# Attention and a bilinear feed-forward layer on one core: the turns of q and k as 64x64 products in four quarters of TensorE

## The chip, the cores and the metric

One core of one Trainium2 chip. The metric is the device time of one execution in microseconds (us). Before the change the median of three runs is 1480.76 us, the lowest 1478.62, the highest 1485.36.

A core has engines that run side by side: TensorE (PE in the profile, with its weight loads listed apart as PEld), VectorE (DVE), ScalarE (ACT), GpSimd (POOL) and the sync engine (SP), whose queue here issues most of the DMAs. A matrix product takes a stationary operand, loaded first, and a moving operand that streams through; its result goes to PSUM, from where another engine copies it.

## The reference

Batch 8, 12 heads, sequence 448, head width 64; then a feed-forward layer over 3584 rows of 768, with inner width 1536.

```python
q_n, k_n = (rmsnorm(q, g_q), rmsnorm(k, g_k))          # over the head width
scores = scale * np.matmul(q_n, k_n.transpose(0, 1, 3, 2))
attn = softmax(scores)                                  # written out in the reference
attn_out = np.matmul(attn, v)
x = attn_out.transpose(0, 2, 1, 3).reshape(3584, 768)
out = ((x @ w_a) * (x @ w_b)) @ w_out
```

q, k, v and the gains are fp32. The three weight matrices are double precision in memory; the kernel loads their words and rounds them itself.

## The kernel before, in words

The program is a list of operations that a planner class (`Plan`) collects and then emits. The order in which they are emitted is written out in a packed constant, `ORDER`; the engines and costs given with each operation are not used to choose an order at build time. Each engine then works through its own instructions in that order and waits on semaphores where it needs another's result.

**Attention.** The work comes in 24 groups `p`: each has four heads of one batch element, as two pairs `w`, each of two heads `h`. For a group, q and k are loaded into tiles of 128 partitions: the pair `w` fills partitions 0 to 63 or 64 to 127 (`low_high[w]`), and each partition holds seven tokens of each head (`NT` = 7 blocks `j` of 64 features). `loads` (L411 on) issues two DMAs a tile on SP, one for each pair; for group 0 one half goes on the ACT queue (L432). q lies as head, then block; k, before the change, as block, then head, so that for every `j` the 128 columns of both heads stand side by side.

`normalize` squares q and k on ACT (L461), adds up on DVE (L463), and takes the inverse root on POOL (L498). q is multiplied by it on DVE (`apply`, L502) into `qn`, which before the change lies as block, then head, like k. k's factor is applied later, as the scale of the exponential (L591).

`transposes` (L523 on) turns k and q so that the head width lies on the partitions. For every block `j` one transpose of 128x128 on TensorE (L537) moves four 64x64 squares (two pairs, two heads), so a turn is seven transposes. The result stands in PSUM in two banks, and ACT copies it to `qkT` (L542 for k, L544 for q with the gain). Group 0 does the same in `turn_first` (L561, L566, L568), with q in two parts and with products on the identity (`warm`, L408) between them, which compute nothing.

`scores` (L585) makes, for each of seven blocks of keys, four products of 64 keys by 448 queries, one in each quarter of the array (64 rows by 64 columns), and ACT takes the exponential into `ET`. `values` (L607) multiplies `ET` by v, again in quarters. The sums over keys come from products with ones (L643), after additions on DVE and POOL (L621) for the later groups.

**Feed-forward.** Between and after the attention, the products with the weights run on the full array (L1292, L869, L1190, L993), on matrices that DVE and ACT combine from the rounded weights (L247 to L256, `factors`). The tiles of k and q are also lent to this part under the same tags (`dF`, `ti`), so their shape appears there again.

The waits of a turn: it needs its input (k's DMA or `qn`), a free `sc` slot in PSUM (two exist, shared with the scores), and so the exponential that reads the slot's last content.

Of the kernel before, what the change touches and what calls it, by code (L numbers as in the profile page):

```python
# [147 lines left out]
def kernel(  # L148
# [126 lines left out]
    def fast_body(ld, wk, ps_s, ps_o, ps_mm, dram):  # L275
# [7 lines left out]
        STS, XS = 2, 9  # L283
        WARM, SPLIT = 4, ((0, 4), (4, NT))
# [129 lines left out]
        def loads(p, nm):  # L414
            b, h0 = p // HC, 4 * (p % HC)
            src = {"q": q, "k": k, "v": v}[nm]
            t = tile_of(f"{nm}{p}", nm, 2 if nm == "v" else 1)

            def emit():
                x = ld.tile([P, NT, 2, D] if nm == "k" else [P, 2, NT * D], FP32, tag=nm, name=nm + "_sb", bufs=2 if nm == "v" else 1)  # L420
                for w in range(2):
                    pair = src[b, h0 + 2 * w:h0 + 2 * w + 2]
                    nc.sync.dma_start(x[low_high[w]], pair.rearrange("h (p j) d -> p j h d" if nm == "k" else
                                                                     "h (p j) d -> p h (j d)", j=NT))
                xs[nm, p] = x
            if p == 0 and nm != "v":
                def begin():
                    xs[nm, p] = ld.tile([P, NT, 2, D] if nm == "k" else [P, 2, NT * D], FP32, tag=nm, name=nm + "_sb", bufs=1)

                def half(w):  # L430
                    pair = src[b, h0 + 2 * w:h0 + 2 * w + 2]
                    queue[("SP", "ACT")[w]].dma_start(  # L432
                        xs[nm, p][low_high[w]], pair.rearrange("h (p j) d -> p j h d" if nm == "k" else "h (p j) d -> p h (j d)", j=NT))
                op(None, 0.0, -11, begin, [], [f"{t}/{w}" for w in range(2)], new=[t])
                for w in range(2):
                    op(("SP", "ACT")[w], 0.7, -10, lambda w=w: half(w), [], [f"{t}/{w}"], kb=350)
                return
            op("SP", 1.28 if nm != "k" else 1.4, p - (1.8 if nm == "v" else 2.0), emit, [f"firsts{PREP}"] if p >= HELD else [], [t], new=[t],
               kb={"q": 690, "k": 770, "v": 530}[nm], dmas=2)
# [4 lines left out]
        def normalize(p):  # L444
# [8 lines left out]
            def squares(s, nm):  # L453
                sq = tile_of(f"sq{nm}{p}", "sq", 1)

                def square():
                    x = xs[nm, p]
                    t = xs["sq", nm, p] = wk.tile([P, 2 * NT, D], FP32, tag="sq", name="sq")
                    flat = (x.rearrange("p h (j d) -> p (h j) d", d=D) if nm == "q" else
                            x.rearrange("p j h d -> p (j h) d"))  # L460
                    nc.scalar.activation(t, flat, AF.Square)  # L461
                op("ACT", 0.95, key, square, loaded(p, nm), [sq], new=[sq])
                op("DVE", 1.1, key, lambda: nc.vector.tensor_reduce(rs[p][:, s], xs["sq", nm, p], AX, ALU.add), [sq], [f"{ms}/{nm}"])  # L463

            def front(n):
# [10 lines left out]
                def times():  # L476
                    if n == 0:
                        qns[0] = wk.tile([P, NT, 2, D], FP32, tag="qn", name="qn")
                    nc.vector.tensor_tensor(
                        qns[0][:, j0:j1].rearrange("p j h d -> p h j d"),  # L480
                        xs["q", 0][:, :, j0 * D:j1 * D].rearrange("p h (j d) -> p h j d", d=D),
                        rs[0][:, 0, a:c].rearrange("p (h j) -> p h j ()", h=2).to_broadcast([P, 2, j1 - j0, D]), ALU.mult)
# [17 lines left out]
            def apply():  # L500
                qns[p] = wk.tile([P, NT, 2, D], FP32, tag="qn", name="qn")
                nc.vector.tensor_tensor(  # L502
                    qns[p].rearrange("p j h d -> p h j d"),
# [19 lines left out]

        def transposes(p):
# [5 lines left out]
            for n, nm in ((1, "k"), (0, "q")):  # L530
                pt = tile_of(f"pt{nm}{p}", "sc", 2)

                def turn(n=n):
                    t = pts[p, n] = ps_s.tile([P, 2 * 512], FP32, tag="sc", name="pt")
                    x = xs["k", p] if n == 1 else qns[p]
                    for j in range(NT):
                        nc.tensor.transpose(t[:, j * P:(j + 1) * P], x[:, j].rearrange("p h d -> p (h d)"), ident)  # L537

                def take(n=n):
                    if n == 1:  # L540
                        qkTs[p] = wk.tile([P, 2, 2 * S], FP32, tag="qkT", name="qkT", bufs=2)
                        nc.scalar.copy(qkTs[p][:, 1], pts[p, 1][:, 0:2 * S])  # L542
                    else:
                        nc.scalar.activation(qkTs[p][:, 0].rearrange("p (w j t) -> p w j t", w=2, j=NT),  # L544
                                             pts[p, 0][:, 0:2 * S].rearrange("p (j w t) -> p w j t", w=2, j=NT),
                                             AF.Copy, scale=gain[:, 0:1])
                op("PE", 0.75, key, turn, [f"{nm}{p}" if n else f"qn{p}", f"half{p - 1}"], [pt], new=[pt], mode="full")
                op("ACT", 0.91 if n else 1.01, key, take, [pt, "gain"], [f"{qkT}/{n}"], new=[qkT] if n else [])

        def turn_first():  # L550

            tile_of("qkT0", "qkT", 2)
            for nm, j0, j1, n in (("k", 0, NT, None), ("q", *SPLIT[0], 0), ("q", *SPLIT[1], 1)):
# [3 lines left out]
                def turn(nm=nm, j0=j0, j1=j1, n=n):  # L557
                    t = pts[0, n] = ps_s.tile([P, 2 * 512], FP32, tag="sc", name="pt")
                    x = xs["k", 0] if n is None else qns[0]
                    for j in range(j0, j1):  # L560
                        nc.tensor.transpose(t[:, (j - j0) * P:(j - j0 + 1) * P], x[:, j].rearrange("p h d -> p (h d)"), ident)  # L561

                def take(j0=j0, j1=j1, n=n):
                    if n is None:
                        qkTs[0] = wk.tile([P, 2, 2 * S], FP32, tag="qkT", name="qkT", bufs=2)
                        nc.scalar.copy(qkTs[0][:, 1], pts[0, None][:, 0:2 * S])  # L566
                    else:
                        nc.scalar.activation(qkTs[0][:, 0].rearrange("p (w j t) -> p w j t", w=2, j=NT)[:, :, j0:j1],  # L568
                                             pts[0, n][:, 0:(j1 - j0) * P].rearrange("p (j w t) -> p w j t", w=2, j=j1 - j0),
                                             AF.Copy, scale=gain[:, 0:1])  # L570
                op("PE", 0.95 * size, -9, turn, (loaded(0, "k") if n is None else [f"qn0/{n}"]) + ["heat"], [pt, "heat"], new=[pt], mode="full")
# [5 lines left out]
        def scores(p, j):  # L577
# [3 lines left out]
            def product():  # L581
                t = scs[p, j] = ps_s.tile([P, 2, 512], FP32, tag="sc", name="sc")
                for w in range(2):
                    for e in range(2):
                        nc.tensor.matmul(t[low_high[w], e, 0:S], lhsT=qkTs[p][low_high[e], 1, j * P + w * D:j * P + (w + 1) * D],  # L585
                                         rhs=qkTs[p][low_high[e], 0, w * S:(w + 1) * S], start=True, stop=True)

            def exps():
                E = ETs[p, j] = wk.tile([P, 2, S], FP32, tag="ET", name="ET", bufs=4)
                for e in range(2):  # L590
                    nc.scalar.activation(E[:, e], scs[p, j][:, e, 0:S], AF.Exp,  # L591
                                         scale=rs[p][:, 1, 2 * j + e:2 * j + e + 1])
# [215 lines left out]
        def deep_products(beta, key, names, h):  # L808
# [30 lines left out]
            def step(m, f, F, names_F):  # L839
# [44 lines left out]
                def first():  # L884
                    pool_, shape = {"k": (ld, [P, NT, 2, D]), "sq": (wk, [P, 2 * NT, D])}.get(tag, (ld, [P, 2, NT * D]))
                    t = pool_.tile(shape, FP32, tag=tag, name="dF", **({"bufs": bufs} if pool_ is ld else {}))
                    F[f] = t.rearrange("p a b c -> p (a b c)" if tag == "k" else "p a b -> p (a b)")
# [224 lines left out]
        def inner_factors(beta, f):  # L1112
# [5 lines left out]
            for k in (slice(0, MI - 1), slice(MI - 1, MI)):  # L1118
                size = (k.stop - k.start) * HI
                quarter = lambda i, j, k=k: (lambda: sts[beta, at][:, i * MI + k.start:i * MI + k.stop, j * HI:(j + 1) * HI])  # L1120
                made = lambda n: (lambda: ts[n])
                for n, x, y, reads in ((2, quarter(1, 1), quarter(0, 1), []), (0, quarter(0, 1), quarter(0, 0), []),
# [3 lines left out]
                    def emit(n=n, x=x, y=y, k=k, size=size):  # L1126
                        t = wk.tile([P, S], FP32, tag="t", name="tk", bufs=2)
                        ts[n] = t[:, 0:size].rearrange("p (k n) -> p k n", n=HI)
                        nc.vector.tensor_tensor(ts[n], x(), y(), ALU.subtract)
                    op("DVE", 0.16 + size / 980, -0.5, emit, [st] + [f"tk{f}.{x}.{k.start}" for x in reads], [nm, "inner factors"], new=[nm], lock=True)  # L1130
                    op("SP", 0.38, 0, lambda n=n, k=k: nc.sync.dma_start(kept["t"][:, f, n, k], ts[n]), [nm], [f"kt{f}.{n}.{k.start}"], kb=0.42 * size)
# [3 lines left out]
        def stream_inner(beta, f):  # L1135
            for n in range(4):
# [3 lines left out]
                def load(n=n, tag=tag, bufs=bufs):  # L1140
                    shape = {"ET": [P, 2, S], "k": [P, NT, 2, D]}.get(tag, [P, 2, NT * D])
                    t = (wk if tag == "ET" else ld).tile(shape, FP32, tag=tag, name="ti", bufs=bufs)
                    flat = t.rearrange("p a b c -> p (a b c)" if tag == "k" else "p a b -> p (a b)")
# [427 lines left out]
```

## Time and profile before

| | |
|---|---|
| median of three runs | 1480.76 us |
| the profiled execution | 1483.82 us |
| its span (first to last instruction) | 1482.0 us |
| TensorE busy | 1459.8 us, 98% of the span, 7886 matmul instructions |
| VectorE, ScalarE, GpSimd busy | 987.5, 437.9, 323.0 us |
| turns of groups 1 to 23 (L537) | 322 matmul instructions |
| DMA packets | 188883, of them under 512 B 62564 |

Busy time of TensorE is the union of instructions in flight; since they are pipelined, their throughput is read from the distance of starts, not from their durations. In the timeline an entry such as `x7` merges seven instructions; its first number is the start of the first and the second the time to the end of the last. A square bracket tells how long the engine stood idle before, and what ended that.

### The profile page before, as it was taken

To read this page: it belongs to the slowest core of one execution; us is meant where nothing else is said; L and a number is where in the kernel's file an instruction comes from. 1 tells how busy PE (TensorE), PEld (TensorE's weight loads), DVE (VectorE), ACT (ScalarE), POOL (GpSimd) and SP (SyncE) were. 2 spreads that over 40 slices of the span, in tenths; PEclk is the share of its full clock that TensorE was granted. 3 is DMA by queue.
4 is the path that set the end of the run, shared out by engine and by line. 5 is a ranking of instruction groups with operands and counts; after the bars stand their busy time and mean duration, and the time that the engine had idled before them with its cause. 6 is when DMAs were issued, how large, how long until landed. Compare 5 with 4: busy or idle time off the path is not lost.

```text
span 1482.0 us, 21059 instructions
## 1 busy us (share of the span) xinstructions
PE 1459.8 (98%) x7886; PEld 960.0 (65%) x7886; DVE 987.5 (67%) x1575; ACT 437.9 (30%) x792; POOL 323.0 (22%) x175
## 2 busy tenths in 40 slices
PE   8999999999999999999999999999999999999998
PEld 5433444555445555555544445799998899999898
DVE  5987799888766233334658765467677766776786
ACT  5878652111464000000257771011111011111100
POOL 3336541120233001101155551011120001111000
PEclk9999999999999999999999999999999999999999
DMA  9885567554443455554656544555555755555464
GB/s 226 221 235 168 123 164 210 187 186 169 159 120 89 155 170 161 178 170 149 180 156 154 128 132 149 165 170 155 161 168 180 251 172 166 159 151 158 160 197 144
DMA packets 188883, 247.99 MB, mean 167 GB/s; under 512 B 62564, under 2 KB 161380, under 8 KB 182116
## 3 DMA queue, kind: packets, MB, share of 16 engines
q1 hardware_dynamic: 159652, 192.61, 45.4%
q10 hardware_dynamic: 29120, 53.94, 10.9%
q8 instruction: 65, 1.06, 0.3%
q14 instruction: 46, 0.38, 0.1%
HBM read 188.35 MB, written 57.93 MB: 166 GB/s over the span
## 4 chain that ended last, share of the span: by engine, by line
PE 84%; DVE 2%; DMA 1%; issue 0%; ACT 0%; SPq 0%; DVEq 0%
PE pq L1292 24%; PE dg L869 17%; PE po L993 16%; PE da L869 6%; PE o L607 5%; PE sc L585 5%; PE a L1190 2%; PE g L1190 2%; PE pt L537 1%; PE b L1190 1%; PE e L1190 1%; PE d L1190 1%; PE su L643 1%; DMA ti<-kept_t 1%; DMA kept_o<-st 0%; DVE x L736 0%
## 5 line engine op out<-in xcount | busy, mean ns | idle before, releaser
L1292 PE MATMUL pq<-x,st 128*128 128x448 f32 x1008 | 384.8, 542 | 2.5 <-DVE t L1333 2.4
L1292 PEld LDWEIGHTS pq<-x,st 128*128 128x128 f32 x1008 | 190.9, 191 | 191.9 <-issue 177.2
L591 ACT ACTIVATE ET<-sc,ms 128x448 f32<-128x448 f32 x336 | 191.0, 637 | 80.3 <-PE sc L585 63.6
L498 POOL TENSOR_TENSOR ms<-ms,expo 128x14 f32<-128x14 f32 x47 | 141.0, 3003 | 117.6 <-DVE ms L496 103.6
L869 PE MATMUL dg<-dT,st 128*128 128x224 f32 x672 | 165.1, 353 | 0.0
L993 PE MATMUL po<-st,hT 128*128 128x384 f32 x492 | 164.2, 488 | 0.0
L869 PE MATMUL dg<-x,st 128*128 128x224 f32 x672 | 163.3, 353 | 0.2 <-DVE dF L916 0.2
L585 PE MATMUL sc<-qkT 64*64 64x448 f32 x1344 | 153.1, 543 | 6.4 <-ACT ET L591 3.4
L607 PE MATMUL o<-ET,v_sb 64*64 64x448 f32 x1344 | 149.3, 540 | 0.0
L897 POOL TENSOR_TENSOR hT<-dF 128x448 f32<-128x448 f32 x42 | 47.1, 1136 | 423.1 <-DVE dF L892 323.0
L993 PEld LDWEIGHTS po<-st,hT 128*128 128x128 f32 x492 | 92.6, 190 | 64.4 <-issue 4.6
L869 PEld LDWEIGHTS dg<-x,st 128*128 128x128 f32 x672 | 126.6, 190 | 2.4 <-DVE dF L916 1.2
L869 PEld LDWEIGHTS dg<-dT,st 128*128 128x128 f32 x672 | 126.6, 190 | 1.4 <-issue 0.2
L621 POOL TENSOR_TENSOR sum<-sum,ET 128x896 f32<-128x896 f32 x40 | 89.0, 2225 | 159.8 <-DVE sum L621 83.2
L869 PE MATMUL da<-x,st 128*128 128x224 f32 x504 | 118.4, 353 | 0.0
L585 PEld LDWEIGHTS sc<-qkT 64*64 64x64 f32 x1344 | 46.3, 132 | 89.8 <-issue 41.3
L607 PEld LDWEIGHTS o<-ET,v_sb 64*64 64x64 f32 x1344 | 49.8, 133 | 72.7 <-issue 64.5
L869 PEld LDWEIGHTS da<-x,st 128*128 128x128 f32 x504 | 94.5, 190 | 1.1
L892 DVE TENSOR_TENSOR dF<-dF 128x896 f32<-128x896 f32 x84 | 92.9, 1106 | 2.5
L621 DVE TENSOR_TENSOR sum<-sum,ET 128x896 f32<-128x896 f32 x60 | 65.3, 1088 | 35.5 <-POOL sum L621 29.2
L882 ACT COPY dt<-da 128x224 f32<-128x224 f32 x84 | 29.1, 346 | 197.5 <-PE da L869 87.1
L993 PE MATMUL po<-st,fin 128*128 128x384 f32 x252 | 86.7, 492 | 0.0
(151 smaller groups left out, 1663.8 us busy)
## 6 DMA issues: line engine op xcount, KB each, us to landing
st<-kept_o SPq DMA_DIRECT2D x28, 1152.0 KB
st<-kept_s SPq DMA_DIRECT2D x84, 320.0 KB
kept<-st ACTq DMA_DIRECT2D x12, 1344.0 KB
st<-kept SPq DMA_DIRECT2D x12, 1344.0 KB
st<-kept SPq DMA_DIRECT2D x84, 192.0 KB
ti<-kept_t SPq DMA_DIRECT2D x48, 288.0 KB
kept_s<-ds SPq DMA_DIRECT2D x30, 448.0 KB
v_sb<-in_v_dram SPq DMA_DIRECT2D x48, 224.0 KB
```

The lines of the kernel that those rows point to most:

```text
L498: lambda: nc.gpsimd.tensor_tensor(msf(), msf(), expo[:, 0:2 * NT * (b - a)], ALU.pow), [], names)
L585: nc.tensor.matmul(t[low_high[w], e, 0:S], lhsT=qkTs[p][low_high[e], 1, j * P + w * D:j * P + (w + 1) * D], rhs=qkTs[p][low_high[e], 0, w ...
L591: nc.scalar.activation(E[:, e], scs[p, j][:, e, 0:S], AF.Exp, scale=rs[p][:, 1, 2 * j + e:2 * j + e + 1])
L607: nc.tensor.matmul(os_[p][low_high[e], w, 0:S], lhsT=xs["v", p][low_high[w], e, j * D:(j + 1) * D], rhs=ETs[p, j][low_high[w], e], start=( ...
L621: two[e].tensor_tensor(sums[p], sums[p] if j > 1 else ETs[p, 0], ETs[p, j], ALU.add)
L869: nc.tensor.matmul(to(), lhsT=W(w), rhs=t(), start=not more and k == 0, stop=k == len(terms) - 1, skip_group_check=True)
L882: nc.scalar.copy(part(0), a())
L892: take("DVE", 1.09, lambda: V.tensor_tensor(F[to], F[to], F[other], ALU.add), allF(other), allF(to), lock=True)
L897: lambda: two[e].tensor_tensor(C(i, n), F[g][:, 0:S], F[g][:, S:2 * S], ALU.mult), allF(g),
L993: nc.tensor.matmul(held["po"][:, 0:HALF], lhsT=a[0]()[:, c], rhs=sts[beta, 12 + place_of[f]][:, c], start=(c == 0), stop=(c == MH - 1))
L1190: nc.tensor.matmul(held[bank], lhsT=x()[:, c], rhs=y(c), start=(start and c == 0), stop=(stop and c == MI - 1), skip_group_check=True)
L1292: nc.tensor.matmul(banks[bank][:, 0:S], lhsT=sts[at][:, f, c * P:(c + 1) * P], rhs=quads[x][:, c], start=(start and c == 0), stop=(stop an ...
```

## The change

Four things change together; the order of operations on every engine stays the same.

1. A turn is no longer seven transposes of 128x128 but 28 products of 64x64 on the identity (`quarter_turns`): for each block `j`, pair `w` and head `h` the 64x64 square is the stationary operand, a 64x64 part of the identity the moving one. The pair picks the array's rows, the head its columns, so the four products of a block use the four quarters.
2. k is loaded as q is: head, then block, so that each partition reads 1792 bytes in a row for each head instead of 256.
3. `qn` is written as head, then block too.
4. The turned tiles lie as pair, then token. ACT reads PSUM as two runs of 448 columns, one in each bank, and `scores` and the exponential's scale index accordingly.

```diff
-                x = ld.tile([P, NT, 2, D] if nm == "k" else [P, 2, NT * D], FP32, tag=nm, ...)
+                x = ld.tile([P, 2, NT * D], FP32, tag=nm, ...)
                 for w in range(2):
                     pair = src[b, h0 + 2 * w:h0 + 2 * w + 2]
-                    nc.sync.dma_start(x[low_high[w]], pair.rearrange("h (p j) d -> p j h d" if nm == "k" else
-                                                                     "h (p j) d -> p h (j d)", j=NT))
+                    nc.sync.dma_start(x[low_high[w]], pair.rearrange("h (p j) d -> p h (j d)", j=NT))
...
-                qns[p] = wk.tile([P, NT, 2, D], FP32, tag="qn", name="qn")
+                qns[p] = wk.tile([P, 2, NT, D], FP32, tag="qn", name="qn")
                 nc.vector.tensor_tensor(
-                    qns[p].rearrange("p j h d -> p h j d"),
+                    qns[p],
...
+        def quarter_turns(t, x, j0, j1):
+
+            for j in range(j0, j1):
+                for w in range(2):
+                    rows = low_high[w]
+                    for h in range(2):
+                        nc.tensor.matmul(t[low_high[h], w, (j - j0) * D:(j - j0 + 1) * D], lhsT=x[rows, h, j * D:(j + 1) * D],
+                                         rhs=ident[rows, rows], start=True, stop=True)
...
-                    t = pts[p, n] = ps_s.tile([P, 2 * 512], FP32, tag="sc", name="pt")
-                    x = xs["k", p] if n == 1 else qns[p]
-                    for j in range(NT):
-                        nc.tensor.transpose(t[:, j * P:(j + 1) * P], x[:, j].rearrange("p h d -> p (h d)"), ident)
+                    t = pts[p, n] = ps_s.tile([P, 2, 512], FP32, tag="sc", name="pt")
+                    quarter_turns(t, xs["k", p] if n == 1 else qns[p].rearrange("p h j d -> p h (j d)"), 0, NT)
...
-                        nc.scalar.copy(qkTs[p][:, 1], pts[p, 1][:, 0:2 * S])
+                        nc.scalar.copy(qkTs[p][:, 1].rearrange("p (w t) -> p w t", w=2), pts[p, 1][:, :, 0:S])
...
-                        nc.tensor.matmul(t[low_high[w], e, 0:S], lhsT=qkTs[p][low_high[e], 1, j * P + w * D:j * P + (w + 1) * D],
+                        nc.tensor.matmul(t[low_high[w], e, 0:S], lhsT=qkTs[p][low_high[e], 1, w * S + j * D:w * S + (j + 1) * D],
```

`turn_first` changes in the same way for group 0. The tiles that borrow k's tag take its new shape, with the same number of elements. The costs that the planner's operations carry for the turns and loads are changed too, which has no effect on the program, since the order is given.

## The prediction

> **What bounds the kernel now.** I read the page first: how busy each engine is, and where.
>
> ```profile
> span 1482.0 us, 21059 instructions
> PE 1459.8 (98%) x7886; PEld 960.0 (65%) x7886; DVE 987.5 (67%) x1575; ACT 437.9 (30%) x792; POOL 323.0 (22%) x175
> PE   8999999999999999999999999999999999999998
> ```
>
> TensorE is busy from end to end; nothing else comes near over the whole span. So any nanosecond taken from or added to TensorE's own stream counts, unless a wait swallows it. From 230 us on TensorE never pauses by this view. Between 20 and 230 us it is at 94 to 96%, with VectorE at 83 to 87%, and short waits of TensorE show (about 10 us in sum): there the engines pull at each other.
>
> Second, the two lines concerned by instruction: the turns (L537) and, for comparison, the score products (L585), which already run in quarters.
>
> ```profile
> L537 PEld LDWEIGHTS pt<-ident,k_sb x161: 137/141/144, 31.3 to 879.0; 128*128 128x128 f32 x161
> L537 PE MATMUL pt<-ident,k_sb x161: 272/273/329, 31.3 to 879.1; 128*128 128x128 f32 x161
> L585 PEld LDWEIGHTS sc<-qkT x1344: 128/133/134, 19.0 to 892.0; 64*64 64x64 f32 x192
> L585 PE MATMUL sc<-qkT x1344: 535/536/588, 19.0 to 892.4; 64*64 64x448 f32 x192
> ```
>
> The counts matter most. 161 is 23 groups x 7 transposes: one pass each. But 24 groups x 7 blocks x 4 products are 672, and the trace has 1344: an fp32 product is two passes, each with its own weight load. What one costs is in the timeline, at a place where TensorE is saturated:
>
> ```profile
> 874.75 0.93 PE L607 MATMUL o<-ET,v_sb 64*64 64x448 f32 x8
> 875.51 0.93 PE L585 MATMUL sc<-qkT 64*64 64x448 f32 x8
> 876.37 2.20 PE L993 MATMUL po<-st,fin 128*128 128x384 f32 x6
> 878.41 0.93 PE L537 MATMUL pt<-ident,k_sb 128*128 128x128 f32 x7
> 879.17 0.93 PE L537 MATMUL pt<-ident,qn 128*128 128x128 f32 x7
> 879.93 2.10 PE L993 MATMUL po<-st,fin 128*128 128x384 f32 x6
> 881.97 0.98 PE L585 MATMUL sc<-qkT 64*64 64x448 f32 x8
> 882.77 0.56 PE L607 MATMUL o<-ET,v_sb 64*64 64x448 f32 x4
> ```
>
> The first column is the start, so differences give throughput. A turn of seven transposes takes 0.76 us (878.41 to 879.17), 0.109 each: 0.85 ns for each of 128 columns. Four products in quarters take 0.75 us (874.75 to 875.51) for two passes of 448 columns: 0.375 a pass, 0.84 ns a column. So a column costs the same in a transpose, in a full pass and in a quarter. From quarters to the full array there is 0.11 us more (875.51 to 876.37 is 0.86), and a product that starts after full-array work takes 0.80 instead of 0.75 (881.97 to 882.77), its first weight load being exposed.
>
> Third, the start:
>
> ```profile
> 1.36 5.22 PE L408 MATMUL warm<-ident 128*128 128x128 f32 x32 [1.36 <-POOL ident masks.py:199]
> 1.51 0.65 ACTq L432 DMA_DIRECT2D k_sb<-in_k_dram  x1
> 1.57 0.83 SPq L432 DMA_DIRECT2D k_sb<-in_k_dram  x1
> 10.81 1.46 PE L561 MATMUL pt<-ident,k_sb 128*128 128x128 f32 x7 [4.23 <-DMA k_sb<-in_k_dram]
> 12.07 3.12 PE L408 MATMUL warm<-ident 128*128 128x128 f32 x16
> 12.99 1.18 DVE L479 TENSOR_TENSOR qn<-q_sb,ms 128x512 f32<-128x512 f32 x2
> 17.14 1.95 PE L408 MATMUL warm<-ident 128*128 128x128 f32 x16
> 19.02 1.36 PE L585 MATMUL sc<-qkT 64*64 64x448 f32 x12
> ```
>
> The first k is awaited 4.2 us, the largest wait of TensorE in the run. It was issued at 1.5 us and used at 10.8, while q, issued at 0.74, was used at 5.6 (L473). The difference is the pattern: k in 14 x 64 pieces of 256 B a half, q in 2 x 64 of 1792 B. In the DMA records a 256 B packet took 27 to 29 ns and a 1792 B one 122 ns: k costs 896 x 28 = 25 us of engine time a half, against 128 x 122 = 16. The wait also let the clock fall: the sixteen warm passes at 12.07 took 3.1 us, those at 17.14 only 1.95.
>
> **What the Trainium skill says.** "TensorEngine Tiling (Array Packing)", Restrictions and Gotchas: column tiling excludes the transpose mode for fp32. So a turn in quarters has to be an ordinary product; this trace shows none in another form. "FP8 and Floating Point Precision", TensorE Precision Notes: true fp32 takes four trips through the array. The trace agrees: 0.84 ns a column in each of two passes, against 0.85 in one for a transpose. "TensorEngine Tiling", Tiling Modes: a change of tiling mode drains TensorE; here 0.11 us.
>
> **The change, part by part.**
>
> *The turn.* Removed: 7 x 0.109 = 0.765 us. Added: 28 products of 64 columns, two passes each: 56 passes over four quarters, 14 one after another in each. A pass of 64 columns is half a full product pass on 128: the sixteen warm passes at 17.14, 276 ns long each, took (1.95 - 0.276) / 15 = 0.112, so 0.056. Bound below: 14 x 64 x 0.84 = 0.75. The weight load bounds it above: 64 columns need some 0.051 us (the 588 of a cold product against 536), and each waits for the pass ahead to start, so 0.059 a pass with a few ns between. Range 0.75 to 0.83; I take 0.80: +0.035 a turn. With 46 turns after the first group: +1.6 us. Half the columns, twice the passes: the four quarters win nothing.
>
> *Switches.* A turn between quarter operations now loses two; one between full ones gains two. I listed the neighbours of the 28 runs of turns: 9 stand between quarters, 8 between full-array work, 11 between one of each. A pair costs about 0.29 us (0.09 going in, 0.09 coming out, two exposed loads of 0.05 to 0.06): 8 - 9 = -1 pair, -0.3 us. Unevenly: before 390 us 7 gain and 1 loses, after it 2 and 7.
>
> *k in whole rows.* First k: same pattern as q, behind q. q's half packets ended at 4.9 us on SP; k's follow, shared with the first weight load (6144 B, 307 ns), so I estimate k usable at 7 to 8.3 instead of 10.8. What is late next: q's roots on POOL end at 10.3 (L489, from 7.34), then qn on DVE to 11.0 to 11.7, q's turns, two copies on ACT of 0.7 and 0.6, scores at about 13.5 to 14.5 instead of 19.0. Warm passes no longer at a low clock help. The gains wait at L222 (10.64) sits behind k on SP and comes forward with it. First exps need k's roots (3 us after q's on POOL: 13.3) and L247, whose raw weights must land first: about 14.5 to 16 instead of 20.1. So -4 to -6 us; I take -5. Of that some is lost before 230 us, where VectorE and ScalarE set waits of their own: I pass on four fifths, -4. Later k loads free about 18 us of engine time each, or 1.1 us on 16 engines; ScalarE waits 2.3 us for k at 29 us. Between 0 and -2; I take 0.
>
> *On the other engines* DVE writes qn straight (L502, 1.09 us), and ACT copies from two banks (0.91 and 1.01 us); same elements, so 0. Should the copies grow by 0.1 us they hide behind TensorE after 230 us; before it up to 2 us would show. No instruction changes place on any queue, and each turn's waits stand at its first products, as before.
>
> Sum: +1.6 - 0.3 - 4 = -2.7 us. The profiled execution, 1483.82 us (span 1482.0), would become 1481.1; the median of 1480.76, 3 us below that execution, becomes **1478**.
>
> **Rivals.**
>
> *It does what it says*: four quarters at once halve a turn, 0.38 to 0.42 us. For it: half the columns. Against: the doubled count at L585. -0.36 x 46 - 4.3 = -21: 1460.
>
> *TensorE can't start 56 small passes so fast* (the slower side). "TensorE: Matmul & The Clock Gate", Wait — 56ns, not 53.3ns, gives 25 ns as the least from start to start. If it holds across quarters, a turn is 56 x 0.025 = 1.4 us: +0.64 x 46 - 4.3 = +25: 1506. Against: in the trace four quarter passes with their loads start 6.7 ns apart; for it: never more than eight before a pause of 0.35 us, where the new turn keeps 14 ns a pass. It decides from 0.86 us a turn (zero in sum); at 1.02 it is 0.5%.
>
> *The start is swallowed*: VectorE, 84% busy from 20 to 230 us, holds the pace, and TensorE stops for it at 222.8 (2.4 us, with the clock down after). Then +1.3: 1482.
>
> *The start carries through and more*: k's faster loads remove waits, and the stop at 222.8 goes (some 4 us with its clock). -6 - 4 + 1.3 - 1: 1471.
>
> **How the numbers follow.** Forecast 0.52, start swallowed 0.15, start and more 0.10, halved turn 0.08, start rate 0.15. Half a per cent, 7.4 us, is about what a measurement here tells from no change. Faster by more: 0.08 + 0.10 + 0.05 of the forecast's own spread = 0.23. Slower by more: 0.14 of the start-rate case (some of it below 1.02 us a turn) + 0.02 = 0.16. Within: 0.61. The range, 1466 to 1492, leaves out the halved turn and most of the start rate. The forecast's own range is 1472 to 1484.
>
> **What would show it.** 112 instructions a turn on TensorE (56 loads, 56 passes). The distance of k's turn to q's, 0.76 now: 0.78 to 0.83 by the forecast, 0.4 by the first rival, 1.4 by the second. First scores at 13.5 to 14.5; no wait for k above 2 us. A turn between products should lose its 0.09 on both sides. I am wrong if the turn isn't near 0.8, or if at 230 us TensorE is no further ahead than it was.

## The result and the profile after

The changed kernel takes 1484.63 us (median of 20 runs, 1482.22 to 1488.08). The kernel before, run beside it, takes 1483.16 us (20 runs, 1478.62 to 1486.19). The ratio is 1.001, with a 95% interval of 1.0003 to 1.0018: 1.5 us slower, little, but with the whole interval above 1, where 2.7 us of gain were forecast. The profiled execution took 1487.31 us (span 1485.5), 3.5 us more than that of the kernel before, so a difference of a microsecond between single traces means nothing by itself. Below, traces serve for places, and ratios for amounts.

The page of the changed kernel:

```profile
span 1485.5 us, 25742 instructions
PE 1464.7 (99%) x10238; PEld 968.6 (65%) x10238; DVE 988.2 (67%) x1575; ACT 438.6 (30%) x792; POOL 325.3 (22%) x175
DMA packets 152037, 248.29 MB, mean 167 GB/s; under 512 B 19556, under 2 KB 124516, under 8 KB 145252
```

TensorE got 2352 more matmul instructions (48 turns, 56 passes in each instead of 7), and is still the one engine that is busy throughout. The small DMA packets went from 62564 to 19556. VectorE, ScalarE and GpSimd have as many instructions as before. (Beside the four things named under The change, the kernel keeps the feed-forward's inner factors under other keys of a Python table, `ts`; the 1575 instructions of VectorE are the same in number.)

The turns by instruction, which answer to the two rows of L537 before:

```profile
L528 PEld LDWEIGHTS pt<-ident,k_sb x1344: 129/135/135, 11.0 to 882.4; 64*64 64x64 f32 x192
L528 PE MATMUL pt<-ident,k_sb x1344: 216/218/267, 11.0 to 882.5; 64*64 64x64 f32 x192
```

1344 for k alone is 24 groups x 7 blocks x 4 squares x 2: the small product is two passes, as its big sister is. The timeline at the place that the prediction showed, the turn of group 23 between two full-array products:

```profile
878.68 0.93 PE L587 MATMUL sc<-qkT 64*64 64x448 f32 x8
879.54 2.20 PE L995 MATMUL po<-st,fin 128*128 128x384 f32 x6
881.67 1.04 PE L528 MATMUL pt<-ident,k_sb 64*64 64x64 f32 x56
882.54 1.00 PE L528 MATMUL pt<-ident,qn 64*64 64x64 f32 x56
883.46 2.20 PE L995 MATMUL po<-st,fin 128*128 128x384 f32 x6
885.60 0.98 PE L587 MATMUL sc<-qkT 64*64 64x448 f32 x8
```

From the first full-array product to the scores it is now 6.06 us (879.54 to 885.60), where it was 5.60 (876.37 to 881.97). Step by step: 2.13 instead of 2.04 until k's turn starts, 0.87 instead of 0.76 for k's turn (its first load is exposed), 0.92 instead of 0.76 for q's turn and the way out, 2.14 instead of 2.04 for the product behind it. This is the costly kind of place: two mode switches that were not there before. Of the 0.46 us, 0.11 are the two turns (0.82 against 0.765 each, see below), and 0.35 the pair of switches.

The other kind is a turn between quarter products. The timeline of the kernel before, at group 1:

```profile
30.42 0.93 PE L607 MATMUL o<-ET,v_sb 64*64 64x448 f32 x8
31.28 0.98 PE L537 MATMUL pt<-ident,k_sb 128*128 128x128 f32 x7
32.23 0.74 PEld L537 LDWEIGHTS pt<-ident,qn 128*128 128x128 f32 x7 [0.20 <-ACT ET L591]
32.23 0.98 PE L537 MATMUL pt<-ident,qn 128*128 128x128 f32 x7
33.14 2.49 PE L607 MATMUL o<-ET,v_sb 64*64 64x448 f32 x24
```

and of the changed kernel:

```profile
31.43 0.93 PE L609 MATMUL o<-ET,v_sb 64*64 64x448 f32 x8
32.18 0.99 PE L528 MATMUL pt<-ident,k_sb 64*64 64x64 f32 x56
32.99 1.00 PE L528 MATMUL pt<-ident,qn 64*64 64x64 f32 x56
33.81 2.44 PE L609 MATMUL o<-ET,v_sb 64*64 64x448 f32 x24
```

Here the whole goes down from 2.72 us (30.42 to 33.14) to 2.38 (31.43 to 33.81). Not all of it is the switches. Before, q's turn starts 0.95 us after k's, 0.19 more than the 0.76 of a turn, and its first weight load had waited for an exponential on ACT (0.20 in the bracket). At group 4, where no such wait shows, the same four steps take 2.54 us before (87.15 to 89.69) and 2.39 after (87.41 to 89.80): 0.15 us gained, the switches' 0.26 less the turns' 0.11. The turn itself takes 0.81 (32.18 to 32.99) and 0.82. Inside a turn the passes of one quarter follow each other every 58 to 59 ns, so 14 of them are 0.82 us.

The start, with the waits that answer to those shown of before (start, time to the end, engine, line, and in brackets the idle time and its releaser):

```profile
10.97 1.04 PE L528 MATMUL pt<-ident,k_sb 64*64 64x64 f32 x56 [3.82 <-DMA k_sb<-in_k_dram]
11.94 3.48 PE L409 MATMUL warm<-ident 128*128 128x128 f32 x16
15.82 0.69 PE L528 MATMUL pt<-ident,qn 64*64 64x64 f32 x32
18.05 2.05 PE L409 MATMUL warm<-ident 128*128 128x128 f32 x16
20.03 1.73 PE L587 MATMUL sc<-qkT 64*64 64x448 f32 x16
```

The first k is used at 10.97 us, not at 7 to 8.3, and the first scores start at 20.03, not at 13.5 to 14.5. Before it was 10.81 and 19.02. Nothing that TensorE waits for at the start came forward.

Why not is in the DMA records. k's half on the SP queue is spread over 16 DMA engines. In the changed kernel ten of them were done by 6.92 us, four more between 7.95 and 9.10, and the last two at 10.88 and 10.93. The half on the ACT queue was complete at 6.25. In the kernel before the engines ended between 8.13 and 10.68. In order of their ends, fourteen are 1.5 to 3.5 us earlier than before and the last two 0.2 us later; and the turn waits for the last one. The DMA columns of the same stretch show it too (window, its length, busy time and count of PE, PEld, DVE, ACT, POOL, then the granted clock, the DMA share, and GB/s):

```profile
7.00:9.00 2.00, 0.15 (x2) 0.00 (x0) 0.40 (x3) 0.00 (x0) 2.00 (x2) 1.00 0.99 301
9.00:11.00 2.00, 0.03 (x4) 0.03 (x4) 0.28 (x2) 0.00 (x0) 0.81 (x1) 1.00 0.69 146
```

While TensorE and ScalarE wait for k, from 9 to 11 us, the DMA engines run out of work (0.69) and carry half of what they did before: most are done, and a few hold everything up. Under way at the same time is the first weight load, 768 KB in 6144-byte packets of some 305 ns each, issued on the ACT queue at 2.26 us. Whether that is what holds the last engines is what e3_first asks.

### The profile page after: what moved, and what is told of

Same layout as the page of the kernel before. It is cut to its first block, busy times and chain, and to the rows that moved or that the text cites. A ratio compares the mean times of both kernels' runs of the same rounds, so it can differ in the third digit from the quotient of the medians.

```text
span 1485.5 us, 25742 instructions
## 1 busy us (share of the span) xinstructions
PE 1464.7 (99%) x10238; PEld 968.6 (65%) x10238; DVE 988.2 (67%) x1575; ACT 438.6 (30%) x792; POOL 325.3 (22%) x175
## 4 chain that ended last, share of the span: by engine, by line
PE 94%; DMA 2%; ACT 2%; DVE 1%; issue 1%; SPq 0%; POOL 0%; ACTq 0%; POOLq 0%
PE pq L1294 26%; PE dg L871 17%; PE po L995 16%; PE sc L587 8%; PE o L609 8%; PE da L871 6%; PE a L1192 2%; PE pt L528 2%; PE g L1192 2%; PE su L645 2%; PE b L1192 1%; PE e L1192 1%; PE d L1192 1%; ACT ET L593 1%; DMA q_sb<-in_q_dram 1%; DMA k_sb<-in_k_dram 1%
```

## The experiments

All ran beside the kernel before; ratios are against it. From every trace the start of each group's first score product was read; the table gives how much later or earlier (us) it lies than in the kernel before, where it lies at 19.0 (group 0), 204.9 (group 10), 381.5 (group 11) and 882.0 us (group 23). The last column is the difference between the last two: what the kernel loses in a stretch with the turns of twelve groups, in which TensorE hardly ever pauses.

Between g10 and g11 the traces differ by something else. Between 218 and 230 us TensorE waits once, 2.2 to 2.5 us, for VectorE, in every trace of the table. In those of the kernel before, the changed one, e3_first, e7_mix and e12_mix_third the granted clock then falls to half for 3.41 us; in the others it does not. One kernel, run twice, shows both (e3_first and e5_first_again). A kernel whose clock did not fall there looks 1.2 to 1.8 us better from g11 on for that alone; g10 and the last column are free of it.

| kernel | turn | k in | first weight load | ratio (95%) | g0 | g10 | g11 | g23 | g11 to g23 |
|---|---|---|---|---|---|---|---|---|---|
| changed kernel | quarters | rows | ACT | 1.001 (1.0003-1.0018) | +1.0 | +0.2 | +0.6 | +3.6 | +3.0 |
| e1_turns | quarters | pieces | ACT | 1.0045 (1.003-1.0059) | +2.1 | +6.6 | +5.0 | +8.0 | +3.0 |
| e2_rows | transposes | rows | ACT | 0.9992 (0.998-1.0005) | -0.8 | +0.5 | -1.2 | -1.2 | 0 |
| e3_first | quarters | rows | SP | 0.9998 (0.9985-1.0012) | -3.0 | -3.2 | -3.1 | -0.3 | +2.8 |
| e5_first_again | quarters | rows | SP | 0.9989 (0.9982-0.9995) | -2.8 | -3.4 | -4.9 | -2.1 | +2.8 |
| e6_before_first | transposes | pieces | SP | 0.9964 (0.995-0.9977) | -4.2 | -1.8 | -3.5 | -3.7 | -0.2 |
| e7_mix | both | both | SP | 0.997 (0.996-0.998) | -2.9 | -4.0 | -3.7 | -3.5 | +0.2 |
| e9_turns_first | quarters | pieces | SP | 1.0013 (1.0003-1.0023) | -3.5 | -2.4 | -4.0 | -0.5 | +3.5 |
| e10_before_first_again | transposes | pieces | SP | 0.998 (0.9972-0.9987) | -4.2 | -4.5 | -6.1 | -6.2 | -0.1 |
| e11_third | quarters | rows | SP | 0.9993 (0.9985-1.0) | -3.9 | -4.3 | -5.5 | -2.7 | +2.8 |
| e12_mix_third | both | both | SP | 0.9974 (0.996-0.9987) | -3.9 | -4.2 | -4.2 | -3.4 | +0.8 |

The last column is the clearest reading of the whole study: kernels that have quarter turns in this stretch lose 2.8 to 3.5 us in it, those that have transposes there between -0.2 and 0.8, whatever the loads do.

**The turns alone** (e1_turns): the changed kernel, with k loaded in 256-byte pieces as before.

```diff
-                x = ld.tile([P, 2, NT * D], FP32, tag=nm, ...)
+                x = ld.tile([P, NT, 2, D] if nm == "k" else [P, 2, NT * D], FP32, tag=nm, ...)
...
-                        nc.tensor.matmul(..., lhsT=x[rows, h, j * D:(j + 1) * D],
+                        nc.tensor.matmul(..., lhsT=x(rows, h, j),          # k: x[rows, j, h]
```

> The turns in quarters alone; k is loaded in pieces of 256 B as before. Theory A (the turn costs TensorE 14 passes of 0.058 us and the loading pattern is worth nothing): as the changed kernel, 1 to 3 us above the kernel before, the distance from k's turn to q's 0.82 to 0.87 us. Theory B (the turn costs more than that, and k's whole rows give some of it back): 4 us or more above the kernel before.

Measured: 1489.17 us (6 runs), 1.0045. In amount this is on the side of the theory in which quarter turns are dear. But the trace puts only 3.0 of the 8 us after group 11. 4.8 us are lost by the group that starts at 72.5 us before, 6.4 by the one at 111.3. Two of TensorE's waits in that part (total, times, longest):

```profile
PE pt L529 <- DMA k_sb<-in_k_dram: 3.0, 1, 3.0
PE o L610 <- DMA v_sb<-in_v_dram: 2.4, 1, 2.4
```

The second stands at 62 us and is not in the trace of before. After this wait the granted clock is at half for 3.41 us (64.9 to 68.3), which costs 1.7 us more; and again from 99.0, behind a wait of 1.98 us for ACT's copy of q. The kernel before has that second wait too, 1.95 us at 94.1, without the fall of the clock. The wait for v and the two falls are 5.8 us, about what is lost by 111.3. So the early loss goes with waits and with the clock after them, not with the speed of the turn; why v came late here and not before, this run doesn't tell.

**The rows alone** (e2_rows): the kernel before, with k's DMAs in whole rows into the same bytes of its tile. The transposes then mix the heads of a block, with the same number of instructions and elements on every engine.

```diff
-                    nc.sync.dma_start(x[low_high[w]], pair.rearrange("h (p j) d -> p j h d" if nm == "k" else ...))
+                    nc.sync.dma_start(x[low_high[w]].rearrange("p j h d -> p (j h d)").rearrange("p (h f) -> p h f", h=2) if nm == "k" else x[low_high[w]],
+                                      pair.rearrange("h (p j) d -> p h (j d)", j=NT))
```

> k in whole rows alone; seven transposes a turn as before. The blocks then mix the two heads, so the scores are others than the reference's; the work is the same in kind and number. Theory A: within 1 us of the kernel before, first k still used at 10 to 11 us. Theory B: 3 to 4 us faster than before.

Measured: 1481.83 us (14 runs), 0.9992, no difference that the interval can tell.

```profile
PE pt L562 <- DMA k_sb<-in_k_dram: 2.3, 1, 2.3
```

k's turn starts at 10.01 us instead of 10.81, and the slowest engine of its SP half ends at 9.88. Whole rows alone don't bring k to 7 or 8 us either. Against this kernel the changed one is 0.18% slower (1.001 to 0.9992), 2.7 us: that is what the quarter turns cost with k in rows, give or take some 2 us, as the two intervals say.

**The first weight load behind k** (e3_first): the changed kernel, with that one DMA issued on SP behind k, the gains and v (at 4.6 us), instead of on ACT at 2.26.

```diff
-                        queue[LOADS].dma_start(to, moe_w_out[k * P:(k + 1) * P, :])
+                        (nc.sync if n == seq[0] and part == 0 else queue[LOADS]).dma_start(to, moe_w_out[k * P:(k + 1) * P, :])
```

> The changed kernel with its first weight load (768 KB) issued on SP behind k, the gains and v, instead of on the ACT queue beside k. If the weight load is what holds k's second half, k is used at 6.5 to 8 us instead of 11.0, and the first scores come at 14 to 16 us instead of 20.0. Theory C (an earlier start carries through): 3 to 5 us faster than the changed kernel. Theory D (it is swallowed before 230 us by the other engines): within 1 us of the changed kernel, with TensorE at 94 us no further ahead.

```profile
7.28 1.04 PE L528 MATMUL pt<-ident,k_sb 64*64 64x64 f32 x56 [0.53 <-DMA k_sb<-in_k_dram]
8.26 2.05 PE L409 MATMUL warm<-ident 128*128 128x128 f32 x16
10.54 0.69 PE L528 MATMUL pt<-ident,qn 64*64 64x64 f32 x32
16.07 1.73 PE L587 MATMUL sc<-qkT 64*64 64x448 f32 x16 [1.25 <-ACT qkT L570]
```

All sixteen engines of k's SP half now end between 6.64 and 7.24 us, k's turn starts at 7.28 instead of 10.97, the warm passes no longer run at a low clock, and the first scores start at 16.07 instead of 20.03. The weight load was what held k; in what way it holds two of sixteen engines so long, the runs don't show. The lead isn't swallowed: it still stands at 4 us against the changed kernel in group 23 (-0.3 against +3.6), and at 220 us the clock fell in both. In time this run, 1482.92 us (14 runs), 0.9998, can't be told from the kernel before; e5_first_again has more runs of it.

**Each turn made twice** (e4_twice): the changed kernel, with the 28 products of every turn issued a second time, to the same result.

```diff
-            for j in range(j0, j1):
+            for j in [*range(j0, j1), *range(j0, j1)]:
```

> The changed kernel with every turn made twice into the same place. If a turn is paid in full everywhere: 46 x 0.82 = 38 us more than the changed kernel. If the 22 turns before 230 us stand beside waits that shrink in turn: 24 x 0.82 = 20 us up to 38. If passes of 64 columns start more slowly when many follow each other: more than 40 us.

Measured: 1550.87 us (5 runs), 1.0459 (1.0441 to 1.0478), 66 us above the changed kernel, beyond what either theory gave. 48 turns x 0.82 us are 39; the rest is a wait that the trace of the changed kernel doesn't have:

```profile
PE pt L528 <- issue: 21.4, 13, 3.1
PE sc L587 <- issue: 4.3, 1, 4.3
```

In the timeline such a pause falls into the middle of a turn, where nothing is waited for:

```profile
864.74 1.81 PE L528 MATMUL pt<-ident,k_sb 64*64 64x64 f32 x112
866.37 0.51 PE L528 MATMUL pt<-ident,qn 64*64 64x64 f32 x18
868.02 1.56 PE L528 MATMUL pt<-ident,qn 64*64 64x64 f32 x92 [1.14 <-issue]
```

Each of these pauses ends 1.2 to 1.7 us after a 16 KB packet of the instruction queue has landed. The likely reading is that TensorE had used up its instructions: 112 passes with their loads in 1.63 us (864.74 to 866.37) are 137 instructions a microsecond. The passes themselves run as in the changed kernel (1.63 us for two turns). So the run confirms 0.82 us a turn, and shows a limit that a single turn (112 instructions) doesn't reach; no trace of the other kernels has such a pause.

**The first weight load behind k, again** (e5_first_again): the kernel of e3_first, unchanged, beside more runs.

> The changed kernel with its first weight load behind k on SP, once more, beside the two that follow on one chip. In the trace of its first run TensorE was 4 us ahead of the changed kernel from the first scores to the end, while the medians of different occasions gave 1.7. If the lead is real: 1478 to 1481 us, or 0.1 to 0.3% faster than the kernel before. If the lead is lost: no difference from the changed kernel, 0.1% slower than before.

Measured: 1481.04 us (21 runs), 0.9989 (0.9982 to 0.9995). The lead at the start reaches group 10 (-3.4); the quarter turns take 2.8 us of it later on, and in the medians 1.6 us of gain are left. Part of it is the clock. The record has the granted clock of every run: 0.9990 on average here, 0.9974 in the kernel before beside it. By estimate that is 0.0016 x 1482 = 2.4 us, no less than the whole gain. In the trace the fall at 12.3 us, behind the wait for k, is gone; in the changed kernel it held TensorE at half speed for 3.41 us.

**The same move on the kernel before** (e6_before_first): the one-line edit of e3_first, on the kernel before.

> The kernel before with nothing but its first weight load moved behind k on SP; k is still in pieces of 256 B and a turn seven transposes. If the weight load alone held k: k used at 7 to 8.5 us, 3 to 4 us faster than the kernel before. If the small pieces are what k needs time for: k used at 9 us or later and less than 2 us gained.

Measured: 1477.9 us (5 runs), 0.9964 (0.995 to 0.9977). k in 256-byte pieces, out of the weight load's way, is complete at 8.11 us on the SP queue, with all engines inside 0.6 us of each other. So the pieces cost about 0.9 us at the start (8.11 against 7.24 in e3_first), and the weight load about 2.6 (10.68 against 8.11).

**Quarter turns in the first half only** (e7_mix): the kernel of e3_first up to group 11; from group 12 on k in pieces and transposes, as before the change.

```diff
+        FULL_FROM = 12
...
+                    if p >= FULL_FROM:
+                        flat, x = t.rearrange("p a b -> p (a b)"), xs["k", p] if n == 1 else qns[p]
+                        for j in range(NT):
+                            nc.tensor.transpose(flat[:, j * P:(j + 1) * P], x[:, j].rearrange("p h d -> p (h d)"), ident)
+                    else:
+                        quarter_turns(t, ...)
```

> Quarter turns and whole rows for groups 0 to 11, where most neighbours are quarter operations; transposes and pieces of 256 B from group 12 on, where most are full-array work; the first weight load on SP. If the quarter turns' loss after 390 us (12 groups, 3 us in the traces) is the passes and the switches: 1475 to 1479 us, 3 us under the same without the transposes, and TensorE keeps to the end the lead it has at group 12.

Measured: 1478.96 us (10 runs), 0.997 (0.996 to 0.998), 2.1 us of median (0.19% by the ratios, 2.8 us) below e5_first_again, which differs from group 12 on alone. The stretch from group 11 to 23 now loses 0.2 us instead of 2.8. This is the quarter turns' price in the part where TensorE is saturated, by time and by place.

**One pass instead of two** (e8_bf16): the changed kernel, in which the turns read only the upper half of every fp32 word, as bf16. It leaves out the lower halves, so q and k are cut to bf16.

```diff
+        def upper(a):
+            return a.bitcast(mybir.dt.bfloat16).rearrange("p (n two) -> p n two", two=2)[:, :, 1]
...
-                        nc.tensor.matmul(..., lhsT=x[rows, h, j * D:(j + 1) * D], rhs=ident[rows, rows], ...)
+                        nc.tensor.matmul(..., lhsT=upper(x[rows, h, j * D:(j + 1) * D]), rhs=upper(ident[rows, rows]), ...)
```

> The changed kernel whose turns read only the upper halves of q, k and the identity, as bf16: the lower bits of q and k are left out, and a product is one pass. If two passes[...] are what makes a quarter turn as long as seven transposes: 7 passes of 0.03 to 0.06 us, 0.2 to 0.41 us a turn, 10 to 25 us faster than the changed kernel. If TensorE cannot start 28 passes faster than one in 25 ns: 0.7 us a turn, 2 to 6 us faster.

Measured: 1469.17 us (4 runs), 0.991 (0.9893 to 0.9927), 1% below the changed kernel. The place of group 23 again:

```profile
861.16 2.20 PE L998 MATMUL po<-st,fin 128*128 128x384 f32 x6
863.29 0.42 PE L531 MATMUL pt<-ident,k_sb 64*64 64x64 bf16 x28
863.54 0.41 PE L531 MATMUL pt<-ident,qn 64*64 64x64 bf16 x28
863.88 2.20 PE L998 MATMUL po<-st,fin 128*128 128x384 f32 x6
```

28 passes instead of 56, and k's turn takes 0.25 us (863.29 to 863.54) instead of 0.87. The four quarters do win, as the first rival had it, once the product is a single pass; passes then also start closer, 31 to 33 ns apart in a quarter once the turn is under way, instead of 58. The whole place takes 4.85 us (861.16 to 866.01, where the scores begin) instead of 6.06. Twelve such groups would be 14.5 us; between groups 11 and 23 the trace is 9 us faster than that of the changed kernel (-10.0 to -16.0, against +0.6 to +3.6). Waits of TensorE that the changed kernel doesn't have there, for ACT and VectorE, take 2.7 us of the rest; what becomes of the other 3 was not followed.

**The turns alone, with the weight load out of the way** (e9_turns_first), and **the load alone once more** (e10_before_first_again): the one-line edit of e3_first on e1_turns, and the kernel of e6_before_first again.

> The quarter turns on k in 256-byte pieces, as in the run of the turns alone (1489.2 us), and the first weight load (768 KB) behind k on SP, as in the run of the kernel before with that load moved (1477.9 us). This closes the square of turn (transpose or quarter) and order of the first load. Theory A: the turns themselves cost 2 to 3 us, after 380 us, in any company, and what the turns alone lost beyond that (about 4 us) came from loads that were late behind each other between 0 and 75 us (v awaited for 2.4 us at 62 us, k for 3.0 at the start). Then with the first load out of the way it takes 1478 + 3 = 1481 us (1479.5 to 1483), its first scores start near 15.5 to 16.5, and between the first scores of the tenth and of the last group it loses 2 to 4 us on the kernel before. Rival: quarter turns on 256-byte pieces cost about 6 us of their own, whatever the loads do: 1484 to 1486 us, with the loss at the same places, by 75 us.

> The kernel before with the first weight load behind k on SP, once more. If its gain is real it again lies at 0.996 to 0.998 of the kernel before, 3 to 5.5 us less; if the first look was luck of the five runs, within 0.1% of it.

Measured: 1484.94 us (21 runs), 1.0013 (1.0003 to 1.0023), and 1479.53 us (19 runs), 0.998 (0.9972 to 0.9987). The move alone gains again. But the two differ by 5.4 us of median, where 3 were expected: in amount the rival (1484 to 1486) was right. Its place was not: nothing is lost by 75 us (the group that starts at 72.5 us before is 1.9 us earlier in e9_turns_first), and the two traces differ by 5.7 us at group 23, and 3.6 of these fall between groups 11 and 23. The other 2.1 lie ahead of group 11, where two traces of one kernel, e6_before_first and e10_before_first_again, already differ by 2.6 us. With k in pieces the quarter turns seem to cost some 2 us more than with k in rows; where, these runs don't settle.

**What held the first scores in e3_first** (e11_third, e12_mix_third). With k there at 7.28, q's copies still came late. ScalarE's timeline in e3_first:

```profile
10.71 0.91 ACT L568 COPY qkT<-pt 128x896 f32<-128x896 f32 x1
14.41 0.34 ACTq L359 DMA_DIRECT2D hraw<-in_moe_w_out_dram  x1
14.86 1.16 ACT L570 ACTIVATE qkT<-pt,gain 128x512 f32<-128x512 f32 x2 [3.24 <-DMA hraw<-in_moe_w_out_dram]
```

q's first part was turned by 11.2 us, but ahead of its copy on ACT stands the issue of the third weight load, and in the trace that issue waits for the semaphore of the second, which it uses again and which was complete at 14.39. With k in pieces the same issue waits on another semaphore and goes out at 11.72 (e6_before_first): the change shifted which DMAs share one. Both kernels move the third load to SP as well, e11_third from e3_first and e12_mix_third from e7_mix:

```diff
-                        (nc.sync if n == seq[0] and part == 0 else queue[LOADS]).dma_start(...)
+                        (nc.sync if (n, part) in ((seq[0], 0), (seq[1], 1)) else queue[LOADS]).dma_start(...)
```

> The changed kernel with the first weight load behind k on SP, as before, and now the third one on SP too, after the q of group 1. With whole rows the third load's issue on ACT waits for the semaphore of the second, which lands at 14.4 us, and the first half of q's turn, ready for ACT's copy at 11.2, is copied only at 14.86 behind it. Theory A: with that issue off ACT's queue the copies run at 11.7 and 13.0, the first scores start at 14.6 to 15.0 instead of 16.1 to 16.3 (the sixteen warm products then end last), and of these 1.4 us about one reaches the end: 1479.5 to 1480.5 us, 0.998 of the kernel before. Rival: something else holds the first scores (the weight load itself, which only moves): they stay at 16 us and the time at 1481.

> The same move of the third weight load in the mixed kernel (quarter turns on whole rows up to group 11, transposes on 256-byte pieces from group 12 on, first weight load on SP), which took 1478.96 us. Theory A: first scores at 14.6 to 15.0 instead of 16.1, 1477.5 to 1478.5 us, and 0.996 of the kernel before. Rival: no change, 1479.

```profile
11.88 0.70 ACT L570 ACTIVATE qkT<-pt,gain 128x512 f32<-128x512 f32 x1
13.28 0.58 ACT L570 ACTIVATE qkT<-pt,gain 128x384 f32<-128x384 f32 x1 [0.70 <-PE pt L528]
15.12 1.74 PE L587 MATMUL sc<-qkT 64*64 64x448 f32 x16
```

In e11_third the copies run at 11.88 and 13.28, and the first scores start at 15.12 instead of 16.1 to 16.3, behind the warm products, which end last now. The wait was what it seemed. About one microsecond of it is still there at group 10 (-4.3 against -3.2 and -3.4). The times don't show it: 1481.72 us (22 runs), 0.9993 (0.9985 to 1.0), and 1478.39 us (7 runs), 0.9974 (0.996 to 0.9987), against 0.9989 and 0.997 without the move. A microsecond is too little for these runs to tell.

**A version that beats both.** The kernel before with only its first weight load behind k was faster than both kernels in both runs (0.9964 and 0.998), by 4.7 and 3.0 us of median. By the same estimate as above about 2 us of each is the clock (0.9988 and 0.9985 on average, against 0.9974 and 0.9971 in the kernel before beside them). Quarter turns up to group 11 and transposes after it, with the same move, are as good (0.997 and 0.9974), not better. Neither is more than 0.4% off the kernel before.

## Why the prediction was wrong

*What bounds the kernel* held: TensorE is at 99%, and what its stream loses or gains after 380 us reaches the end.

*The turn* held. Forecast 0.80 us from 0.056 to 0.059 us a pass; measured 0.82 from 58 to 59 ns, and 0.81 to 0.82 from one twin to the next in e4_twice. 46 x (0.82 - 0.765) is 2.5 us, where 1.6 stood.

*The switches* held, in size and place. The forecast priced a pair at 0.29 us (0.09 in, 0.09 out, two exposed loads) and put five more pairs lost than gained after 390 us. Measured, a pair is 0.26 at group 4 and 0.35 at group 23. With 24 turns at 0.055 the forecast's pairs make 1.3 + 1.5 = 2.8 us after group 11; the six fp32 kernels with quarter turns throughout and once each lose 2.8 to 3.5 there. That the early part gains pairs is to be seen at group 4 (2.54 to 2.39 us), but not in the time: from group 0 to group 10 the changed kernel gains 0.8 us in the trace, and that only makes up for its later start.

*The start* is the step that failed: "k's follow, shared with the first weight load (6144 B, 307 ns), so I estimate k usable at 7 to 8.3 instead of 10.8". It came at 10.97. The weight load was named in that sentence, but the estimate shows no price for it and takes k for one stream, while a load is complete when the last of its sixteen parts is. Most parts did keep the estimate (eleven of sixteen by 8 us); five did not. The 4 us credited to the start were 0. The rest of the sum, +1.3, is close to the +1.5 measured, with some luck: its turns were 0.9 us too cheap, and +2.2 would have stood there. Without the weight load k is usable at 7.28, inside the forecast. Even then the first scores came at 16.1 and not at 13.5 to 14.5, because of ScalarE's wait for a DMA semaphore, which the prediction did not see; without that as well they start at 15.1, behind warm products. "No instruction changes place on any queue" was true and still not enough: the waits that come with the DMAs' semaphores did change (the third weight load's issue uses the second's semaphore after the change, and another one before).

*Later k loads at 0* held within the noise (e2_rows 0.9992).

*The rivals.* A halved turn: no, for an fp32 product; yes for one in a single pass (e8_bf16). A start rate of 25 ns for all quarters together, 1.4 us a turn: no, the quarters together start a pass every 14.6 ns. The 25 ns that the "TensorE: Matmul & The Clock Gate" page of the Trainium skill gives (section Wait — 56ns, not 53.3ns) doesn't hold across quarters by this trace; within one quarter no run here goes below it (58 ns in fp32, 31 in bf16). Its neighbour, too few instructions in time, shows only at twice the load (e4_twice). The start swallowed: its number (1482, +1.3 in the sum) came out, for another reason. Where k came earlier, most of the lead was carried as a rule: at group 10 e5_first_again still has 3.4 us and e10_before_first_again 4.5, though e6_before_first only 1.8 of its 4.2. The start didn't lose its gain on the way; it never made one. The start carrying more: no. The stop at 222.8 us stays, at 2.2 to 2.5 us in every trace of the table, whatever k does; the fall of the clock behind it comes and goes from one execution to the next.

*The skill's other statements.* The drain at a change of tiling mode ("TensorEngine Tiling (Array Packing)", Tiling Modes) held: the traces show 0.09 to 0.11 us a side. That an fp32 product takes four passes ("FP8 and Floating Point Precision", TensorE Precision Notes) is not what the traces count. They have two for each product, and the prediction's "the trace agrees" says too much: a column at 0.84 ns in each of two passes shows two. The two together, 2 x 58 ns in a quarter, take about as long as three and a half of e8_bf16's passes, at 31 to 33 ns.

The forecast's last sentence named its own refutation: "if at 230 us TensorE is no further ahead than it was". At 205 us it was 0.2 us behind.

## What to carry to other kernels

A load is there when its slowest engine is done: before crediting a better pattern, look at how far apart the engines end and what else is on them, on other queues too; moving one 768 KB load by 2 us did more here than a sevenfold longer piece. Count passes, not columns, when a transpose is to become a product: here, in fp32, two passes in quarters cost a little more than one transpose on the full array (0.82 against 0.765 us a turn), and the mode switches decide the rest. And where a change touches DMAs, compare the waits of every issue, since here a DMA's issue waited for the one that had used its semaphore, and a copy behind it on ScalarE waited with it for 3.2 us. And before a difference of one or two microseconds between two traces is explained, look at the granted clock: one fall is worth 1.7 us, and the same kernel has it in one execution and not in the next.

## What the runs showed of the hardware

- TensorE paused with nothing to wait for when each turn was made twice: at 137 instructions a microsecond, 14 times, for 26 us in all (e4_twice). Each pause ended 1.2 to 1.7 us after a 16 KB instruction packet had landed, as if it had run out of instructions. The changed kernel, with 112 instructions in 0.82 us and slower work between, never paused so.
- Four quarters together start a pass with its weight load every 14.6 ns over a whole turn (58 to 59 ns in each quarter for fp32), and every 9 ns in bf16 (0.25 us for 28).
- DMA engines under mixed load end far apart: 6.34 to 10.93 us for the sixteen parts of one 224 KB load, when a load with 6144-byte packets on another queue was under way, and 6.64 to 7.24 when it was not.
- The granted clock falls to half for 3.41 us behind some waits of TensorE and not behind others of the same length: behind 2.4 us at 222.8 us in the kernel before, behind 1.98 us at 98.9 us in e1_turns; not behind 2.5 us at 218.9 us in e11_third, nor behind 1.95 us at 94.1 us in the kernel before. Each fall costs 1.7 us.
